# Attention pairs with pooled PSUM tiles, a reordered gate chain in the first expert layer, and one 512 column w2 operand in the second

## The chip, the cores and the metric

One core of a Trainium2 chip runs the whole program. The metric is the device time of one execution in microseconds (us), lower is better. Time before: 1605.31 us, the median of 3 runs (1603.46 to 1607.17).

## The reference

Three layers, all in float32. Attention over 4 batches of 2496 rows, with squared ReLU in place of softmax; then two mixture-of-experts layers over the 9984 rows that come out, each row going to the one expert of 8 with the largest logit.

```python
# attention: u, v (4, 2496, 256), z (4, 2496, 64)
attn = np.maximum(z @ z.transpose(0, 2, 1) / S, 0) ** 2
x = (u * (attn @ v)).reshape(B * S, D)
# layer 1: only rows with x @ w_skip > 0 are computed, the others pass through
e = argmax(xc @ w_gate);  g = softmax(xc @ w_gate)[e]
out = xc + g * (np.maximum(xc @ w1[e], 0) @ w2[e])       # w1 (8, 256, 1024), w2 (8, 1024, 256)
# layer 2: every row; logits get a bias by modality; no residual
out = g * (np.maximum(x @ w1[e], 0) @ w2[e])
```

## The kernel before, in words

To reach float32 accuracy on TensorE each operand is split into a high and a low part (`hh`, `hl`, `w2h`, `w2l`, `ah`, `al`, ...), and a product is three matmuls: high by high, high by low, low by high. ScalarE (ACT) makes the high part by a copy, VectorE (DVE) or GpSimd (POOL) subtracts it for the low part. The program orders the work of every engine by hand, and each engine runs its instructions in the order in which the code emits them.

**Attention.** A unit is two key tiles of 128 against a chunk of up to 512 queries; 4 batches of 5 chunks of 10 units make 200 units. In unit i TensorE does `scores` of unit i and `values` of unit i - 3 (`LAG`); ACT does ReLU (L285) and square (L297), DVE the cast (L298) and the low part (L299). `jobs` puts loads and splits of the next batch's z and v at written units. When a chunk's `values` are done, its `tail` generator runs one step a unit, emitted after the unit's own split and jobs: product with u, high and low part of the rows (`xh` L350, `xl` L351), four steps `rows(g)` that transpose the rows and multiply them by both gates on TensorE (L365) and copy the result out (L369, L373), then the argmax (`FirstMax`, `first_max_done`, L114 to L141), exp (L123), and the ranks: `row_index` has eight small matmuls (L153, L158, L163) that need the last sum of L141, and after DVE work the rows are scattered to lists in DRAM, one list per expert of either layer (L687). The small PSUM results live in `Banks`, one tile of two banks whose halves are handed out in turn.

**Expert layers.** `Moe1` takes 348 rows of one expert in a turn, `Moe2` 512. A turn (`turn`, `work`) is eight steps `hidden(f)` (six matmuls each, L767, then ReLU on ACT, L769, and the low part on DVE, L770) and eight steps `out_part(f)` (L868 in Moe1, L978 in Moe2). A plan, keyed ("h", f) or ("o", f), says what is emitted behind each step: "next" loads the next turn's rows and w1, "w1" b and "w2" b split a quarter of a weight (ACT, with DVE for w1 and POOL for w2, L672 and L673), "x" d transposes the next rows (L752), "after" runs one step of the generator that finishes the turn before. `Moe1.after` copies y out of PSUM (L878, L879), makes yl (L882), multiplies by the second gate (L886, L888), transposes y back and adds it to the rows (`x_out`, L895, L899), then does logits (L905), argmax, and ranks; `send` scatters `x_out` (three indirect DMAs on POOL, L687). POOL instructions `touch` (L709) take the waits for the DMAs; the one in `index` stands ahead of DVE's write of the row numbers `ix` (L713). `Moe2.out_part` has the 128 rows as the stationary operand and 256 columns of w2 as the moving one.

Of the kernel before, what the change touches and what calls it, by code (L numbers as in the profile page):

```python
# [183 lines left out]
class Attention:  # L184
# [51 lines left out]
    def z_split(self, b, i):  # L236
# [97 lines left out]
    def tail(self, b, c):  # L334
# [17 lines left out]
        yield  # L352

# [3 lines left out]
        def rows(g, lo=lo):  # L357

            ps = self.ps_m.both()
            q = slice(g * 128, g * 128 + 128)  # L360
            for d in range(2):
                cc = slice(64 * d, 64 * d + 98)
                for i, m in enumerate((xh, xl)):
                    for h, p in enumerate(HALVES):
                        nc.tensor.matmul(  # L365
                            ps[:, h, cc], m[p, d, q], self.wg[p, d, cc], start=(d == i == 0), stop=(d == i == 1),
                            skip_group_check=True,
                        )
# [45 lines left out]
    def run(self, first, inits, late):  # L414
# [32 lines left out]
        for b in range(nb):  # L447
# [4 lines left out]
            if b + 1 < nb:  # L452
                for i, (c, u) in enumerate(((1, 9), (2, 7), (2, 9), (3, 7), (3, 9))):
# [3 lines left out]
                for g, (c, u) in enumerate(((4, 5), (4, 7), (4, 9), (5, 4), (5, 6))):  # L457
# [155 lines left out]
class Banks:  # L613


    def __init__(self, pool):
        self.t, self.i = pool.tile([128, 2, 512], F32, name="m"), 0

    def both(self):
        return self.t  # L620

    def tile(self, shape, dtype, name):
        t = self.t[:shape[0], self.i]
        self.i = 1 - self.i
        if len(shape) == 2:
            return t[:, 0:shape[1]]
        return t[:, 0:shape[1] * shape[2]].rearrange("p (a b) -> p a b", a=shape[1])


class Shared:  # L630


    def __init__(self, ctx, tc, w):
# [9 lines left out]
        self.ps_m = Banks(pool("ps_m", 1, space=PSUM))  # L643
# [4 lines left out]
    def more(self, ctx):  # L648
# [3 lines left out]
        self.hi.append([p.tile([128, 2, 256], F32R, name=f"w2h{b}") for b in range(4)])  # L652
        self.lo.append([p.tile([128, 2, 256], F32R, name=f"w2l{b}") for b in range(4)])
# [70 lines left out]
class Moe:  # L724
# [68 lines left out]
    def turn(self, follow, after, hooks=None):  # L793
# [4 lines left out]
        def hook(what, *args):  # L798
# [10 lines left out]
            elif what == "x":  # L809
                nxt[0].x_transposed(args[0])  # L810
            elif what == "load w2":
# [12 lines left out]
class Moe1(Moe):  # L824
    PLAN = {
        "start": [("next",), ("after",)],
        ("h", 0): [("after",)],
        ("h", 1): [("after",)],
        ("h", 2): [("w2", 0)],
        ("h", 3): [("w2", 1)],  # L830
        ("h", 4): [("w2", 2), ("after",), ("after",)],
        ("h", 5): [("w2", 3), ("load w2",), ("after",)],
        ("h", 6): [("after",)],
        ("h", 7): [("after",)],
        ("o", 0): [("x", 0)],
        ("o", 1): [("w1", 0), ("after",)],
        ("o", 2): [("w1", 1)],
        ("o", 4): [("x", 1), ("w1", 2)],
        ("o", 5): [("w1", 3), ("after",)],
# [30 lines left out]
    def after(self, lim, current, ps=None):  # L870
# [17 lines left out]
        nc.scalar.copy(lt[:2 * E], lt_ps)  # L888
        yield
        x, xo = self.x_cur, self.x_out[:P]  # L890
        for g0 in range(0, G, 2):
# [10 lines left out]
            yield  # L902
        lg_ps = sh.ps_m.tile([128, G, 128], F32, name="m")[:P]
        for g in range(G):
            nc.tensor.transpose(lg_ps[:, g], lt[:, g * P:(g + 1) * P], k.ident)  # L905
        lo = s.tile([128, G, 2 * E], F32, name="mlo")[:P]
        nc.scalar.copy(lo, lg_ps[:, :, 0:2 * E])
        lg = s.tile([128, G, E], F32, name="mlg")[:P]
        nc.vector.tensor_tensor(lg, lo[:, :, 0:E], lo[:, :, E:], op=ALU.add)
        nc.vector.tensor_tensor(lg, lg, x[:, :, C_G1:C_G1 + 1].to_broadcast([P, G, E]), op=ALU.mult)  # L910
        nc.vector.tensor_tensor(lg, lg, x[:, :, C_B2:C_B2 + E], op=ALU.add)
        yield
        fm = FirstMax(nc, s, k, lg, P, G, "b")
        fm.exp()
        oh, sm = fm.hot, fm.total()
        nc.vector.tensor_copy(xo[:, :, C_TID], x[:, :, C_TID])
        nc.vector.reciprocal(xo[:, :, C_G2], sm)
        yield
        if current is not None:
            self.load_rows(current(), self.x_cur)  # L920
        nc.vector.tensor_copy(sh.lim, lim.rearrange("p t o -> p (t o)"))
        mk = self.counted(sh.lim)
        ohb, cum = first_max_done(nc, s, k, oh, mk, P, 1, G, "b")
        yield
        at, mk = row_index(nc, s, ps or sh.ps_m, k, ohb, cum, mk, self.carry, P, 1, G, "b")
        self.sc.index(at[:, 0], mk[:, 0])
# [11 lines left out]
class Moe2(Moe):  # L938
    PLAN = {
        "start": [("next",), ("after",)],  # L940
        ("h", 2): [("after",)],
# [20 lines left out]
    def take_y(self):  # L962
        self.y = [y[:, :D] for y in self.sh.y] + [self.sh.ps_m.tile([128, D], F32, name="m") for _ in range(2)]
# [238 lines left out]
```

## Time and profile before

| | |
|---|---|
| median of 3 runs | 1605.31 us |
| the profiled execution, its own time | 1608.57 us |
| its span from first to last instruction | 1606.8 us |
| busy: PE, weight loads, DVE, ACT, POOL | 1503.0, 1315.0, 1052.0, 940.8, 633.1 us |
| mean granted clock of TensorE | 0.982 |

PE is TensorE's matmuls, PEld its weight loads. Matmuls overlap, and their ends are modelled, so a busy PE can still have pauses of under 0.15 us. An arrow in a row names what ended a wait. SP is the queue that issues most loads.

### The profile page before, as it was taken

How to read it: one execution, taken by the hardware profiler on the slowest of the kernel's cores; microseconds unless marked ns; L12 is line 12 of the kernel's file. 1: busy time of each engine (PE TensorE's matmuls, PEld its weight loads, DVE VectorE, ACT ScalarE, POOL GpSimd, SP SyncE). 2: the span in 40 equal slices, each digit the busy share in tenths (PEclk: the TensorE clock that was granted, in tenths of full speed). 3: DMA queues.
4: the chain of work that ended last, by engine and by line, in shares of the span. 5: the costliest groups of instructions: out<-in, count | busy, mean ns of one | idle time of the engine just before them, and what ended most of it. 6: DMA issues, size and time to landing. Idle time of an engine off the chain costs nothing. (4 is left out here: it accounts for less than half of the span.)

```text
span 1606.8 us, 35550 instructions
## 1 busy us (share of the span) xinstructions
PE 1503.0 (94%) x11612; PEld 1315.0 (82%) x11612; DVE 1052.0 (65%) x2466; ACT 940.8 (59%) x1577; POOL 633.1 (39%) x740
## 2 busy tenths in 40 slices
PE   6999999999999999999779888889999999999996
PEld 4888887778888888888678887888989998998995
DVE  7688787878778787777656665656644454454442
ACT  7676777767677776665355444544454555455442
POOL 4222233333222222335444345553544544454453
PEclk9999999999999999999899999999999999999998
DMA  4611111112111110031355445553434433433430
GB/s 141 227 41 60 56 39 43 44 62 85 39 35 66 54 41 27 30 92 43 102 157 156 139 139 146 155 155 107 152 122 154 148 114 131 155 116 119 157 118 22
DMA packets 49694, 160.23 MB, mean 100 GB/s; under 512 B 13285, under 2 KB 15195, under 8 KB 40384
## 3 DMA queue, kind: packets, MB, share of 16 engines
q1 hardware_dynamic: 28432, 124.19, 24.6%
q0 software_dynamic: 20736, 34.71, 6.3%
q8 instruction: 61, 1.00, 0.3%
q14 instruction: 33, 0.27, 0.1%
q10 hardware_dynamic: 432, 0.07, 0.0%
HBM read 124.24 MB, written 46.55 MB: 106 GB/s over the span
## 5 line engine op out<-in xcount | busy, mean ns | idle before, releaser
L687 POOL DMA_INDIRECT rows<-r,ix x160 | 203.4, 1272 | 294.5 <-DVE ah L298 153.4
L328 PE MATMUL o<-ah,vh 64*128 64x512 f32 (+1 forms) x1560 | 312.7, 387 | 4.5 <-DVE xs L341 4.3
L770 DVE SCALAR_TENSOR_TENSOR hl<-ph,hh 128x512 fp32r<-128x512 f32 (+1 forms) x288 | 176.7, 615 | 213.9 <-ACT hh L769 212.9
L328 PE MATMUL o<-al,vh 64*128 64x512 f32 (+1 forms) x1560 | 305.5, 386 | 0.0
L328 PE MATMUL o<-ah,vl 64*128 64x512 f32 (+1 forms) x1560 | 304.1, 386 | 0.0
L285 ACT ACTIVATE t<-s 128x1024 f32<-128x1024 f32 (+2 forms) x201 | 200.7, 999 | 108.5 <-PE s L282 98.6
L769 ACT ACTIVATE hh<-ph 128x512 fp32r<-128x512 f32 (+1 forms) x288 | 155.1, 539 | 185.9 <-PE ph L767 172.2
L299 DVE TENSOR_TENSOR al<-t,ah 128x1024 fp32r<-128x1024 f32 (+2 forms) x201 | 244.6, 1217 | 18.3 <-PE m L365 0.5
L673 POOL TENSOR_TENSOR w2l<-w2raw,w2h 128x512 fp32r<-128x512 f32 x144 | 183.4, 1288 | 169.5 <-issue 132.2
L767 PE MATMUL ph<-mxh,zA 128*128 128x512 f32 (+1 forms) x576 | 217.4, 377 | 10.0 <-PEq L1198 5.6
L298 DVE CAST ah<-t 128x1024 fp32r<-128x1024 f32 (+2 forms) x201 | 140.2, 697 | 113.3 <-ACT t L297 111.0
L767 PE MATMUL ph<-mxh,zB 128*128 128x512 f32 (+1 forms) x576 | 212.0, 368 | 0.0
L767 PE MATMUL ph<-mxl,zA 128*128 128x512 f32 (+1 forms) x576 | 211.9, 368 | 0.0
L297 ACT ACTIVATE t<-t 128x1024 f32<-128x1024 f32 (+2 forms) x201 | 208.0, 1035 | 5.7
L328 PEld LDWEIGHTS o<-ah,vh 64*128 64x128 f32 x1560 | 152.1, 187 | 37.7 <-DVE xs L341 8.7
L328 PEld LDWEIGHTS o<-al,vh 64*128 64x128 f32 x1560 | 151.9, 186 | 27.7
L328 PEld LDWEIGHTS o<-ah,vl 64*128 64x128 f32 x1560 | 148.3, 186 | 28.5
L767 PEld LDWEIGHTS ph<-mxh,zA 128*128 128x128 f32 x576 | 110.7, 192 | 25.4 <-issue 8.2
L282 PE MATMUL s<-zA,zB 64*128 64x512 f32 (+1 forms) x400 | 124.7, 390 | 0.0
L282 PE MATMUL s<-zB,zA 64*128 64x512 f32 (+1 forms) x400 | 122.9, 390 | 0.0
L767 PEld LDWEIGHTS ph<-mxh,zB 128*128 128x128 f32 x576 | 110.3, 192 | 14.8
L767 PEld LDWEIGHTS ph<-mxl,zA 128*128 128x128 f32 x576 | 110.6, 192 | 13.9
(235 smaller groups left out, 3274.1 us busy)
## 6 DMA issues: line engine op xcount, KB each, us to landing
w1raw<-in_w SPq DMA_DIRECT2D x36, 1024.0 KB, 7.6
w2raw<-in_w SPq DMA_DIRECT2D x36, 1024.0 KB, 9.5
x_in<-rows SPq DMA_DIRECT2D x20, 520.0 KB
vraw<-in_v SPq DMA_DIRECT2D x20, 512.0 KB, 4.0
ut<-in_uT SPq DMA_DIRECT2D x20, 512.0 KB, 4.8
x_in<-rows SPq DMA_DIRECT2D x16, 364.3 KB
x_cur<-rows SPq DMA_DIRECT2D x16, 364.3 KB
rows<-x_in POOLq DMA_DIRECT2D x8, 536.0 KB, 8.2
```

What stands on the lines that cost most here:

```text
L282: nc.tensor.matmul(s[:, i, :n], w[p, k], x[p, q], start=(j == 0), stop=(j == 2))
L285: nc.scalar.activation(t[:, i, :n], s[:, i, :n], AF.Relu, scale=SCALE)
L297: nc.scalar.activation(t[:, i, :n], t[:, i, :n], AF.Square)
L298: nc.vector.tensor_copy(h[:, i, :n], t[:, i, :n])
L299: nc.vector.tensor_tensor(l[:, i, :n], t[:, i, :n], h[:, i, :n].bitcast(F32), op=ALU.subtract)
L328: nc.tensor.matmul(o[half][d][:, :n], w[p, d * 128:d * 128 + 128], x[p, :n], start=(u == 0 and j == at[0]), stop=(u == 9 and j == at[-1]),)
L673: lo_engine.tensor_tensor(l, src, h.bitcast(F32), op=ALU.subtract)
L687: i = tc.nc.gpsimd.indirect_dma_start(out=out, out_offset=bass.IndirectOffsetOnAxis(ap=ix, axis=0), in_=rows, in_offset=None, bounds_check ...
L767: nc.tensor.matmul(ps, w, x, start=(i == 0), stop=(i == len(mms) - 1))
L769: nc.scalar.activation(h, ps, AF.Relu)
L770: nc.vector.scalar_tensor_tensor(l, ps, 0.0, h.bitcast(F32), op0=ALU.max, op1=ALU.subtract)
```

## The change

- Attention: the copy of the last 64 columns of z goes from ACT to DVE. The tail gets an empty step ahead of `rows`, so all that follows comes a unit later; exp, ranks and the index now stand in one step, with the sums, reciprocals and scatters in the next. `Banks` is gone: `ps_m` is a pool of two one-bank tiles, and each `rows(g)` is copied out by four ACT copies in place of two. Four of five splits of z and three of v move to an earlier unit, one of v to a later one.
- Moe1: `after` has the gate chain (lt, logits, argmax, exp, ranks, index) first, then the transposes of y and the rows. y stays in PSUM longer: yl is computed from it, and the copies to `yS` follow the lt matmuls. `send` leaves the start of the turn for ("h", 3) of the next one; w2 quarters 0 and 1 are split at ("o", 6) and ("o", 7) of the turn before, 2 and 3 at ("h", 1) and ("h", 2), and the load of the next w2 follows there.
- Moe2: w2's high and low part lie side by side, so one matmul of 512 columns takes both for `hh`, and a second of 256 columns adds `hl` by the high part to the upper half. `after` then adds the two halves with four more DVE instructions.

```diff
-                nc.scalar.copy(t[:, S:S + 64], t[:, S - 64:S].bitcast(F32))
+                nc.vector.tensor_copy(t[:, S:S + 64], t[:, S - 64:S].bitcast(F32))
...
         yield
+        yield
...
-            ps = self.ps_m.both()
+            ps = [self.ps_m.tile([128, 196], F32, name="m") for _ in HALVES]
...
-            nc.scalar.copy(
-                r[:, g, 0:D].rearrange("p (d h c) -> p h d c", d=2, h=2),
-                ps[:, :, 0:196].rearrange("p h (d c) -> p h d c", d=2)[:, :, :, 0:64],
-            )
-            nc.scalar.copy(lo[:, :, g], ps[:, :, 64:98])
+            to = r[:, g, 0:D].rearrange("p (d h c) -> p d h c", d=2, h=2)
+            for h, t in enumerate(ps):
+                nc.scalar.copy(to[:, :, h], t.rearrange("p (d c) -> p d c", d=2)[:, :, 0:64])
+                nc.scalar.copy(lo[:, h, g], t[:, 64:98])
...
         fm.exp()
-        yield
-        sm = fm.total()
         at, mk = row_index(nc, self.p_s, self.ps_m, k, ohb, cum, mk, self.carry, 128, 2, 4, "a")
...
+        yield
+        sm = fm.total()
...
-                for i, (c, u) in enumerate(((1, 9), (2, 7), (2, 9), (3, 7), (3, 9))):
+                for i, (c, u) in enumerate(((1, 8), (2, 5), (2, 8), (3, 5), (3, 8))):
...
-                for g, (c, u) in enumerate(((4, 5), (4, 7), (4, 9), (5, 4), (5, 6))):
+                for g, (c, u) in enumerate(((4, 5), (4, 6), (4, 8), (5, 5), (5, 7))):
...
 class Moe1(Moe):
     PLAN = {
         "start": [("next",), ("after",)],
         ("h", 0): [("after",)],
-        ("h", 1): [("after",)],
-        ("h", 2): [("w2", 0)],
-        ("h", 3): [("w2", 1)],
-        ("h", 4): [("w2", 2), ("after",), ("after",)],
-        ("h", 5): [("w2", 3), ("load w2",), ("after",)],
+        ("h", 1): [("after",), ("w2", 2)],
+        ("h", 2): [("w2", 3), ("load w2",)],
+        ("h", 3): [("send",), ("after",)],
+        ("h", 5): [("after",)],
         ("h", 6): [("after",)],
         ("h", 7): [("after",)],
-        ("o", 0): [("x", 0)],
-        ("o", 1): [("w1", 0), ("after",)],
-        ("o", 2): [("w1", 1)],
-        ("o", 4): [("x", 1), ("w1", 2)],
-        ("o", 5): [("w1", 3), ("after",)],
+        ("o", 0): [("x", 0), ("after",)],
+        ("o", 1): [("w1", 0)],
+        ("o", 2): [("after",), ("w1", 1)],
+        ("o", 3): [("after",)],
+        ("o", 4): [("after",), ("x", 1), ("w1", 2)],
+        ("o", 5): [("w1", 3)],
+        ("o", 6): [("w2", 0)],
+        ("o", 7): [("w2", 1)],
     }
...
         for d in range(2):
-            nc.scalar.copy(y[:, d], self.y[d])
             nc.scalar.copy(yh[:, d], self.y[d])
         for d in range(2):
             yield
-            nc.vector.tensor_tensor(yl[:, d], y[:, d], yh[:, d].bitcast(F32), op=ALU.subtract)
+            nc.vector.tensor_tensor(yl[:, d], self.y[d], yh[:, d].bitcast(F32), op=ALU.subtract)
...
         nc.scalar.copy(lt[:2 * E], lt_ps)
+        for d in range(2):
+            nc.scalar.copy(y[:, d], self.y[d])
         yield
...
     with tc.For_i(0, n, 1, iteration_sync=mode) as j:
-        m1.send()
         m1.turn(lambda: m1.next(j), m1.finish(j))
...
 class Moe2(Moe):
...
-            for i, (h, w) in enumerate(((self.hh, wh), (self.hl, wh), (self.hh, wl))):
-                nc.tensor.matmul(
-                    self.y[g][:P], h[f][:, gg], w, start=(f == 0 and i == 0), stop=(f == 7 and i == 2)
-                )
+            nc.tensor.matmul(
+                self.y[g][:P], self.hh[f][:, gg], w.rearrange("p t d -> p (t d)"), start=(f == 0), stop=False
+            )
+            nc.tensor.matmul(self.y[g][:P, D:], self.hl[f][:, gg], w[:, 0], start=False, stop=(f == 7))
...
+        for g in range(G):
+            if g % 2 == 0:
+                yield
+            nc.vector.scalar_tensor_tensor(
+                self.o[:P, g], self.y[g][:P, D:], old[:P, g, 0:1], self.o[:P, g], op0=ALU.mult, op1=ALU.add
+            )
```

The plans of the turns that are not in a loop follow the same order.

## Rows read from the trace of the kernel before

**Rows 1.** Busy time by stage: start:end us, length, engines, granted clock, DMA share, GB/s

```profile
0.00:752.60 752.60, 719.29 (x6646) 595.35 (x6646) 592.46 (x1223) 533.23 (x732) 232.72 (x211) 0.99 0.19 64
...
812.70:1093.70 281.00, 242.14 (x1535) 229.36 (x1535) 175.15 (x585) 139.79 (x326) 131.50 (x169) 0.98 0.50 147
1093.70:1141.90 48.20, 44.80 (x289) 40.06 (x290) 33.82 (x112) 23.41 (x50) 23.64 (x33) 1.00 0.39 134
1141.90:1554.00 412.10, 412.10 (x2635) 373.22 (x2635) 199.18 (x393) 207.59 (x388) 194.97 (x259) 1.00 0.41 134
```

**Rows 2.** Waits of PE, whole span: us in total, times, longest us

```profile
PE m L895 <- DVE x_out L899: 26.2, 14, 3.6
PE s L282 <- ACT t L285: 15.6, 7, 3.8
PE m L895 <- ACT mlt L888: 14.0, 16, 1.0
PE m L365 <- DVE xl L351: 7.6, 25, 0.7
...
PE m L153 <- DVE mxl L757: 6.5, 3, 5.5
```

**Rows 3.** Waits of all engines, the two behind those of PE

```profile
DVE x_out L899 <- DMA rows<-x_out,ix_scatter: 28.8, 13, 4.6
...
ACT zA L248 <- DVE zA L244: 14.0, 4, 3.6
```

**Rows 4.** Stretches before and in a drop of the granted clock, columns as in rows 1

```profile
161.00:163.00 2.00, 0.04 (x5) 0.00 (x0) 0.58 (x1) 1.36 (x5) 0.00 (x0) 1.00 0.00 0
163.00:166.50 3.50, 3.49 (x18) 2.90 (x20) 2.35 (x6) 2.81 (x3) 0.00 (x0) 0.51 0.00 0
...
907.10:910.60 3.50, 2.88 (x12) 2.81 (x13) 1.47 (x4) 0.37 (x1) 1.21 (x2) 0.51 0.40 87
```

**Rows 5.** Timeline of one tail's ranks, DVE and PE: start, duration, instruction

```profile
229.34 0.21 DVE L114 TENSOR_REDUCE mxa<-lg 128x8 f32<-128x64 f32 x1
...
231.18 0.77 DVE L141 TENSOR_TENSOR cuma<-cuma,ohba 128x16 bf16<-128x16 bf16 x4
231.20 0.39 PE L282 MATMUL s<-zA 64*128 64x512 f32 x1
...
234.60 0.20 PE L153 MATMUL m<-ohba,tri 64*128 64x64 bf16 x2
```

**Rows 6.** Groups by line, ACT copies of rows: count, busy us, mean ns, idle before

```profile
L369 ACT COPY r<-m 128x256 f32<-128x256 f32 x80 | 29.8, 372 | 46.5 <-PE m L365 45.5 <-issue 0.4
L373 ACT COPY lo<-m 128x68 f32<-128x68 f32 x80 | 17.8, 223 | 0.0
```

**Rows 7.** Timeline of one loop turn of Moe1, begun at 833.69, all engines

```profile
839.22 1.27 POOL L687 DMA_INDIRECT rows<-x_out,ix_scatter  x1 [0.18 <-PE m L886]
...
840.51 4.98 POOL L673 TENSOR_TENSOR w2l<-w2raw,w2h 128x512 fp32r<-128x512 f32 x4
...
842.10 0.48 DVE L899 SCALAR_TENSOR_TENSOR x_out<-m,x_cur 116x256 f32<-116x256 f32 x1 [2.27 <-DMA rows<-x_out,ix_scatter]
...
843.77 0.43 PE L895 MATMUL m<-ident,yS 128*116 128x128 f32 x2 [1.99 <-DVE x_out L899]
```

**Rows 8.** The tile x_out: its scatters, from issue to landing

```profile
DMA to landing us min/median/max: 4.0/4.4/5.0
```

**Rows 9.** The line of the splits, DVE: ns min/median/max, first and last start

```profile
L673 DVE TENSOR_TENSOR zB<-w1raw,zA x140: 678/685/1434, 772.2 to 1563.6; 128x512 fp32r<-128x512 f32 x140
```

**Rows 10.** DMA issues of the page: KB each, median us to landing

```profile
w2raw<-in_w SPq DMA_DIRECT2D x36, 1024.0 KB, 9.5
```

**Rows 11.** Timeline of PE in Moe2: neighbours of 256 columns, then of 512

```profile
1306.09 0.28 PE L978 MATMUL m<-w2h,hh 128*128 128x256 f32 x1
1306.21 0.28 PE L978 MATMUL m<-w2h,hl 128*128 128x256 f32 x1
...
1309.26 0.39 PE L767 MATMUL ph<-mxh,zA 128*128 128x512 f32 x1
1309.49 0.40 PE L767 MATMUL ph<-mxl,zA 128*128 128x512 f32 x1
```

More of the change, by code (lines that the diff above doesn't have):

```diff
@@ L651, in more @@
         p = self.p = pool("moe", 1)
-        self.hi.append([p.tile([128, 2, 256], F32R, name=f"w2h{b}") for b in range(4)])
-        self.lo.append([p.tile([128, 2, 256], F32R, name=f"w2l{b}") for b in range(4)])
+        self.w2hl = [p.tile([128, 2, 2, D], F32R, name=f"w2{b}") for b in range(4)]
+        self.hi.append([t[:, :, 0] for t in self.w2hl])
+        self.lo.append([t[:, :, 1] for t in self.w2hl])
         self.hh = [p.tile([128, 512], F32R, name=f"hh{f}") for f in range(8)]
@@ L810, in hook @@
                 nxt[0].x_transposed(args[0])
+            elif what == "send":
+                self.send()
             elif what == "load w2":
@@ L888, in after @@
         nc.scalar.copy(lt[:2 * E], lt_ps)
+        for d in range(2):
+            nc.scalar.copy(y[:, d], self.y[d])
         yield
         x, xo = self.x_cur, self.x_out[:P]
+        lg_ps = sh.ps_m.tile([128, G, 128], F32, name="m")[:P]
+        for g in range(G):
+            nc.tensor.transpose(lg_ps[:, g], lt[:, g * P:(g + 1) * P], k.ident)
+        lo = s.tile([128, G, 2 * E], F32, name="mlo")[:P]
+        nc.scalar.copy(lo, lg_ps[:, :, 0:2 * E])
+        lg = s.tile([128, G, E], F32, name="mlg")[:P]
+        nc.vector.tensor_tensor(lg, lo[:, :, 0:E], lo[:, :, E:], op=ALU.add)
+        nc.vector.tensor_tensor(lg, lg, x[:, :, C_G1:C_G1 + 1].to_broadcast([P, G, E]), op=ALU.mult)
+        nc.vector.tensor_tensor(lg, lg, x[:, :, C_B2:C_B2 + E], op=ALU.add)
+        yield
+        fm = FirstMax(nc, s, k, lg, P, G, "b")
+        yield
+        nc.vector.tensor_copy(sh.lim, lim.rearrange("p t o -> p (t o)"))
+        mk = self.counted(sh.lim)
+        ohb, cum = first_max_done(nc, s, k, fm.hot, mk, P, 1, G, "b")
+        yield
+        fm.exp()
+        yield
+        at, mk = row_index(nc, s, sh.ps_m, k, ohb, cum, mk, self.carry, P, 1, G, "b")
+        self.sc.index(at[:, 0], mk[:, 0])
+        yield
         for g0 in range(0, G, 2):
@@ L901, in after @@
                 )
[L902 to L915, printed above, removed]
+            if g0 == 0:
+                yield
         nc.vector.tensor_copy(xo[:, :, C_TID], x[:, :, C_TID])
-        nc.vector.reciprocal(xo[:, :, C_G2], sm)
-        yield
+        nc.vector.reciprocal(xo[:, :, C_G2], fm.total())
         if current is not None:
             self.load_rows(current(), self.x_cur)
[L921 to L926, printed above, removed]
     def send(self):
@@ L940 @@
         "start": [("next",), ("after",)],
+        ("h", 0): [("after",)],
+        ("h", 1): [("after",)],
         ("h", 2): [("after",)],
@@ L962, in take_y @@
     def take_y(self):
-        self.y = [y[:, :D] for y in self.sh.y] + [self.sh.ps_m.tile([128, D], F32, name="m") for _ in range(2)]
+        self.y = self.sh.y + [self.sh.ps_m.tile([128, 2 * D], F32, name="m") for _ in range(2)]
     def x_transposed(self, d):
@@ L992, in after @@
         for g in range(G):
-            nc.scalar.activation(self.o[:P, g], self.y[g][:P], AF.Copy, scale=old[:P, g, 0:1])
+            nc.scalar.activation(self.o[:P, g], self.y[g][:P, :D], AF.Copy, scale=old[:P, g, 0:1])
+        for g in range(G):
+            if g % 2 == 0:
+                yield
+            nc.vector.scalar_tensor_tensor(
+                self.o[:P, g], self.y[g][:P, D:], old[:P, g, 0:1], self.o[:P, g], op0=ALU.mult, op1=ALU.add
+            )
         yield
@@ L1080, in forward_kernel @@
         "start": [("next",), ("after",)],
+        ("h", 0): [("after",)],
         ("h", 2): [("after",)],
@@ L1136, in forward_kernel @@
         "start": [("after",)],
-        ("h", 0): [(lambda: m2.table.spread(nc, sh.ps_x, k),), ("next",)],
+        ("h", 0): [("after",), (lambda: m2.table.spread(nc, sh.ps_x, k),), ("next",)],
     })
```

54 lines of the change are left out of this document (22 added, 32 removed).

## The prediction

> **What bounds the kernel now.** I read the busy time by stage first [rows 1]. PE is busy 719 of 753 us in attention, 412 of 412 in Moe2's stage, but only 242 of 281 in the 13 loop turns of Moe1; DVE, the next engine, has 592, 199 and 175. So PE sets the time everywhere, and an edit is worth what it takes from PE's own work or from PE's waits. The list of PE's waits [rows 2] says where the waits are: those on `x_out` and `mlt` are Moe1's (40 us together), those on `t` and `xl` attention's (23 us). Behind them [rows 3] stand the scatter that must have read `x_out` before it is written again, and ACT's wait of about 3.5 us for DVE in each of the four z splits. Last I looked at the granted clock [rows 4]: after 2 us without a matmul at 161 it is 0.51, the level of 1.2 GHz, for 3.4 us, which costs 1.7 us. I count such stretches: four in attention (37, 163, 347, 532), each behind a wait of PE of 2 to 4 us, and four in Moe1's loop (907, 931, 996, 1081).
>
> **Attention, what goes.** The copy of z's last columns on DVE: ACT no longer stands 3.5 us in its queue ahead of the next ReLU, for which PE waits [rows 2, 3]. At the three changes of batch that is 2.0 us of wait and 1.7 us of slow clock each, 11 us; in batch 0 the wait is the longest row, 3.8, of which I take 3.3 (another split stays in ACT's queue there) and 1.7, so 5 us. DVE's two copies of 64 columns are small beside its 1.2 us subtractions. The empty step gives `xl` a whole unit more: all 25 waits of L365 go, 7.6 us by the row, 8 as ends are modelled. Sum -24. The four ACT copies for two: by the two rows [rows 6] a copy is about 0.17 us plus 0.8 ns a column, so 0.93 us for 0.60 a step, 80 steps, 27 us of ACT. ACT is at 533 of 753, and the copies fall into the 1.1 us in which it waits for the next scores: nothing. If that cover went, it would be up to 0.3 us a step, 27 us.
>
> **Attention, what comes.** Between the argmax and the rank matmuls the old tail has two units of PE work, the new one has one. In the tail of [rows 5] the argmax starts at 229.34, which is ReLU, square, cast and subtraction behind the unit's start, and its last sum ends at 231.95; PE is at the place of the rank matmuls, one unit earlier than today's 234.60, at 231.20. So PE, in order, stands 0.75 us, and 0.06 for the release. I took the same difference at 18 tails: 0.72 to 1.22 us, more where a split of z or v falls just ahead, as it now does in four of five chunks. Mean 1.0, 19 tails, +19 us. Queued behind are the next unit's scores, and ACT, DVE behind these. The bounds: 0, if DVE ran the argmax earlier than I think, and 2.7 us a tail if each stall brought the slow clock. Waits of PE for `xs` of up to 0.85 us brought none, so I take the stall alone. Attention: -5.
>
> **Between attention and the experts** the two early transposes of Moe1's rows now take a small PSUM tile between two `rows` steps, and the next of these waits for DVE's `mxl`: some 2.2 us, perhaps with a slow stretch; the wait of L153 for `mxl` [rows 2] stays in part. +4 (0 to 8).
>
> **Moe1's loop.** 281.0 us by 13 turns is 21.6 [rows 1]. PE's own work is 242.1 / 13 = 18.6, and 18.1 without the four slow stretches (6.8 us). The wait of 1.9 us a turn is that for `x_out` [rows 2, 7]: the rows are sent at the turn's start, the third scatter goes out at 839.22, 5.5 us into the turn, and `x_out` is written again from 842.10, so DVE waits, and PE's second pair of transposes with it. The other, 0.9, is the transposes behind `mlt`. In the new order the rows are written behind ("o", 3), some 9 us after the send, and the transposes of `lt` come two steps after its matmuls: both waits go. What is late next is the send itself. POOL must first do w2 quarters 2 and 3, 1.25 us each [rows 7], behind ACT's copies for ("h", 1) and ("h", 2): low parts done at 4.4 and 5.6 us into the turn, touches 1.1, scatters at 6.7, 8.6 and 10.3, and the last lands 4.4 to 5.0 us later [rows 8], at 14.7 to 15.3. The index step, behind ("o", 2) at 12.5, has a POOL touch that waits for it, and DVE waits for the touch. DVE's queue behind: w1 quarter 1 (0.69), three `x_out` (0.48), the sums and small copies (0.7), `mxl` (0.52): done at 18.4, when the next turn needs it at 18.1 + 0.6. So it just fits; two w1 quarters are still to do, and these meet w2 quarters 0 and 1 on POOL. The DVE split takes 685 ns, but up to 1434 [rows 9], and 18 of 140 take twice the time, those beside POOL's subtraction of w2. That is up to 1.5 us more in DVE's queue, of which the low parts of the next turn's hidden steps can pass on part to PE through three PSUM tiles. I take 18.5 us a turn, from 18.1 (nothing passed on) to 20.
>
> SBUF — State Buffer, section Who interferes with whom, in the Trainium skill, says that a DVE instruction with two SBUF inputs contends with a GpSimd instruction that reads SBUF; the doubled split times agree. It speaks against the new place of quarters 0 and 1: by it both splits would be doubled in each turn, and if all of that reached PE it would be 13 x 1.5 = 20 us, about the first rival's time.
>
> The load of w2 goes out at 5.6 and takes 9.5 [rows 10]: 15.1, and it is needed at 16.7. Loop: 13 x 18.5 and 1.9 for leaving it, 242.4, so -38.6. The two turns behind the loop have 48.2 - 44.8 = 3.4 us of idle PE [rows 1]: -3.4.
>
> **Moe2.** Each pair of a row group and a quarter step is now 512 + 256 columns for 3 x 256. Neighbours stand 0.12 us apart at 256 columns and 0.23 at 512 [rows 11]: 0.35 for 0.36. 32 pairs in 20 turns, 640 in all, by some 8 ns: -5 us. The bounds: 512 columns at twice 0.12 give 0; at 2.4 GHz without any extra they take 0.213, -17 us. The saved weight loads are hidden behind matmuls today. The four DVE additions (about 0.48 each as for `x_out` [rows 7], 1.9 a turn) go to DVE at 199 of 412: nothing, but +0.5 in the last turn, where nothing follows.
>
> TensorE: Matmul & The Clock Gate, section Back-to-back issue gap, in the Trainium skill, gives N / 2.4 + 2.5 ns from one matmul to the next. That is 109 and 216 ns where the trace has 120 and 230; by it the pair would save 2.5 ns, 1.6 us in all.
>
> **The sum.** -5 + 4 - 38.6 - 3.4 - 5 + 0.5 = -47.5. The profiled execution took 1608.6, so 1561; it was 3.3 above the median, so against 1605.3 I say **1558 us**.
>
> **Rivals.**
> - *The send is the new bound of Moe1.* Landing and the doubled splits make a turn 20.3. For it: the margin I find is a few tenths. Against: 4.4 us is a narrow row. 13 x 1.8 more: 1581. Chance 0.13.
> - *The rank stalls pull the clock down.* 19 x 1.7 = 32 more: 1590. For: PE stands once a chunk. Against: nothing of 0.85 us did it. 0.06.
> - *No rank stall*, as DVE is early: 19 less, 1539. For: DVE has one step less to do in a unit. Against: [rows 5]. 0.10.
> - *Slower than before.* The one way that I see: the scatters land behind the w2 load, which now runs beside them, and the touch holds DVE until a turn is over 22.2 us, that is a landing 3.7 us later than 15. Each us costs 13, and from there the loop gives back all; at 22.5 it is 1610. Against: today's w1 load runs beside the scatters too, and they land in 5.0 at most. 0.06.
> - *The wide operand gives nothing*: 512 columns cost twice 256. 1563, inside my forecast's own range, 1545 to 1572, which has 0.62.
> - No change at all, several things cancelling: 0.03.
>
> The range reaches to the first rival and nearly to the third: 1536 to 1586. A measurement of this kernel tells about 0.2% from no change. Faster 0.90, same 0.03, slower 0.07.
>
> **What would show it.** The waits of L365 for `xl` and of L248 gone, and the clock full at the batch changes; a new wait of PE at L153 of about 1 us, 19 times. Loop turns of 18 to 19 us without waits at L895; a wait of DVE at L713 or of POOL's touch for the scatter near 13 to 15 us into the turn. L978 at 0.23 and 0.12. Wrong I am if DVE's queue in Moe1 passes its lateness on to L767, or if the slow clock follows the new stalls.

## The result: slower by 1%, and the profile after

| | before | after |
|---|---|---|
| median | 1609.1 us (8 runs, 1603.5 to 1616.6) | 1623.4 us (8 runs, 1620.9 to 1626.5) |
| ratio | | 1.0101, 95% interval 1.0081 to 1.0121 |
| span of the profiled execution | 1606.8 us | 1619.1 us |
| mean granted clock of TensorE | 0.982 | 0.975 |

I had forecast 1558 us, 1536 to 1586. The time lies outside the range, and on the other side of no change.

The stages of the changed kernel, by windows cut at the same places of the program as in [rows 1] (columns as there):

```profile
0.00:748.50 748.50, 720.01 (x6646) 606.97 (x6646) 602.70 (x1231) 541.34 (x876) 231.10 (x211) 1.00 0.20 64
748.50:811.90 63.40, 45.28 (x262) 41.27 (x262) 38.47 (x124) 23.77 (x64) 29.97 (x33) 0.84 0.35 101
811.90:1100.90 289.00, 246.01 (x1534) 235.03 (x1535) 191.60 (x585) 140.83 (x326) 130.85 (x169) 0.95 0.51 144
1100.90:1153.30 52.40, 47.77 (x256) 42.21 (x257) 36.03 (x113) 22.07 (x48) 23.43 (x33) 0.92 0.38 127
1153.30:1565.40 412.10, 409.40 (x2092) 345.34 (x2091) 224.47 (x464) 206.30 (x388) 192.89 (x257) 1.00 0.40 134
```

Against [rows 1], attention is 4.1 us shorter and Moe1's loop 8.0 us longer, where I had 38.6 shorter. The two turns ahead of the loop take 63.4 for 60.1 us, the two behind it 52.4 for 48.2, Moe2's stage the same 412.1. With 0.9 us more at the end, that is the 12.3 us between the spans. So the bulk of the miss is Moe1's loop: 289.0 us for the 242.4 of the prediction, 46.6 us too long. All that lies outside the loop comes out 13.2 us above its forecasts.

PE's waits over the whole span of the changed kernel, beside [rows 2]:

```profile
PE m L737 <- DMA x_in<-rows: 29.8, 13, 4.7
PE ph L752 <- DVE mxl L742: 13.1, 7, 2.0
PE ph L752 <- PEq L1202: 12.2, 2, 7.6
PE m L158 <- DVE cuma L141: 8.1, 20, 0.4
PE s L282 <- ACT t L285: 7.8, 7, 2.6
PE m L153 <- DVE cuma L139: 6.7, 8, 4.0
...
PE m L153 <- DVE cumb L139: 3.3, 1, 3.3
PE m L366 <- DVE mxl L742: 3.3, 1, 3.3
...
PE m L366 <- DVE xl L351: 0.2, 1, 0.2
```

Moe1's two old waits (`x_out` 26.2, `mlt` 14.0) are gone, as forecast. In their place PE waits for the next rows: 29.8 us for the load of `x_in` and 13.1 for the low part of such rows. In the loop alone (813 to 1101) the list is this, 43.1 us in all:

```profile
PE m L737 <- DMA x_in<-rows: 20.9, 11, 2.5
PE ph L752 <- DVE mxl L742: 13.1, 7, 2.0
PE ph L752 <- PEq L1202: 7.6, 1, 7.6
PE ph L752 <- DVE hl L755: 1.5, 3, 0.5
```

The clock adds to it. In the loop TensorE stands at the lower of its two levels, 1.2 GHz, for 29.1 us in eight stretches (from 812, 846, 891, 935, 966, 1021, 1065 and 1096), each of them in or behind one wait of PE of 2.0 to 7.6 us; in the kernel before it is 13.7 us in four. This is the stretch at 891, behind a wait of 2.5 us:

```profile
890.90:894.30 3.40, 3.40 (x16) 3.33 (x15) 1.21 (x2) 1.71 (x4) 0.00 (x0) 0.50 0.41 146
```

By the price of [rows 4], 1.7 us for 3.4, that is an estimate of 14.5 us, for 6.8 before.

Who is behind the waits stands in the list of all engines' waits (L694 is the POOL touch, L698 DVE's write of the index):

```profile
POOL ix_scatter L694 <- DMA rows<-x_out,ix_scatter: 80.8, 15, 7.0
...
ACT zA L657 <- DMA w1raw<-in_w: 25.0, 15, 8.9
DVE ix_scatter L698 <- POOL ix_scatter L694: 24.9, 14, 2.4
```

The touch waits for the scatters' landing, and DVE waits for the touch, 1.8 us a turn. The turns of the loop alternate: six take 19.2 to 21 us and seven 21.7 to 26.7, the last of which leaves the loop. One of the shorter, begun at 855.39, and the start of the next (begun at 875.93), from the timeline:

```profile
858.67 2.54 POOL L658 TENSOR_TENSOR w<-w2raw,w 128x512 fp32r<-128x512 f32 x2 [0.78 <-issue]
...
861.44 0.34 SPq L649 DMA_DIRECT2D w2raw<-in_w  x1
...
865.79 1.27 POOL L672 DMA_INDIRECT rows<-x_out,ix_scatter  x1 [0.19 <-issue]
...
874.09 0.18 POOL L694 TENSOR_TENSOR ix_scatter<-ix_zero_scatter 1x3 int32<-1x3 int32 x1 [7.03 <-DMA rows<-x_out,ix_scatter]
874.31 0.16 DVE L698 TENSOR_TENSOR ix_scatter<-atb,mk 116x3 int32<-116x3 f32 x1 [2.20 <-POOL ix_scatter L694]
875.02 1.26 DVE L912 SCALAR_TENSOR_TENSOR x_out<-m,x_cur 116x256 f32<-116x256 f32 x3
876.89 0.31 SPq L730 DMA_DIRECT2D x_cur<-rows  x1
879.53 0.30 SPq L730 DMA_DIRECT2D x_in<-rows  x1
...
890.41 0.49 PE L737 MATMUL m<-ident,x_in 116*128 116x116 f32 x3 [2.46 <-DMA x_in<-rows]
```

The third scatter goes out at 10.4 us into the turn (I had 10.3) and lands 8.1 us later, at 18.5 (I had 14.7 to 15.3); the touch that waits for it starts at 18.7. In the other turns the third scatter goes out at 10.4 to 13.9 us, later in most of the longer ones, whose first steps wait for the low part of their rows, and the touch starts at 17.1 to 20.9. DVE writes the index 2.2 us late, so the sums of `x_out` come late, so `x_cur`, which they read, is loaded late. On SP `x_in` stands behind `x_cur`: it goes out 3.6 us into the next turn, where PE wants it at its first output step and stands 2.5 us. The scatters of `x_out` from issue to landing, beside [rows 8]:

```profile
DMA to landing us min/median/max: 4.1/7.5/9.5
```

The busy share of the 16 transfer engines in tenths, in 40 slices over the 24 us from the start of a turn (the turn and the start of the next), first in the kernel before (942.5 on), then in the changed one (855.4 on):

```profile
DMA  2969999966746321000009589983122222259899
```

```profile
DMA  1022222999999999999887532222200000000311
```

The share over the loop is the same (0.50 and 0.51), but before it came in bursts apart: w1 and the scatters first, w2 in the middle, the rows' loads at the end. Now `x_in`, w1, w2 and the scatters share one burst of some 9 us, and then the engines are idle for 5.

### The profile page after: what moved, and what is told of

Its sections match the earlier page's. It is cut to its first block, busy times and chain, and to the rows that moved or that the text cites. A ratio compares the mean times of both kernels' runs of the same rounds, so it can differ in the third digit from the quotient of the medians.

```text
span 1619.1 us, 34652 instructions
## 1 busy us (share of the span) xinstructions
PE 1505.8 (93%) x10972; PEld 1301.7 (80%) x10972; DVE 1111.8 (69%) x2554; ACT 949.0 (59%) x1729; POOL 632.3 (39%) x740
## 5 line engine op out<-in xcount | busy, mean ns | idle before, releaser
L672 POOL DMA_INDIRECT rows<-r,ix x160 | 202.6, 1266 | 269.1 <-DVE xs L341 205.9
L658 POOL TENSOR_TENSOR w<-w2raw,w 128x512 fp32r<-128x512 f32 x144 | 187.3, 1311 | 249.5 <-issue 153.8
L752 PE MATMUL ph<-mxh,zA 128*128 128x512 f32 (+1 forms) x576 | 216.3, 375 | 21.2 <-PEq L1202 12.2
L752 PE MATMUL ph<-mxl,zA 128*128 128x512 f32 (+1 forms) x576 | 213.9, 371 | 13.1 <-DVE mxl L742 13.1
L298 DVE CAST ah<-t 128x1024 fp32r<-128x1024 f32 (+2 forms) x201 | 146.5, 729 | 97.9 <-ACT t L297 94.7
L328 PEld LDWEIGHTS o<-ah,vl 64*128 64x128 f32 x1560 | 151.9, 185 | 24.7
L741 ACT CAST mxh<-m 128x512 fp32r<-128x512 f32 (+1 forms) x72 | 37.8, 525 | 176.0 <-PE m L737 170.4
L858 PE MATMUL o<-hh,w 128*128 128x348 f32 x512 | 137.1, 352 | 0.5 <-POOL w L658 0.5
L658 DVE TENSOR_TENSOR zB<-w1raw,zA 128x512 fp32r<-128x512 f32 x140 | 114.8, 840 | 28.7 <-ACT zA L657 23.1
```

Source lines behind the costliest of these rows:

```text
L298: nc.vector.tensor_copy(h[:, i, :n], t[:, i, :n])
L328: nc.tensor.matmul(o[half][d][:, :n], w[p, d * 128:d * 128 + 128], x[p, :n], start=(u == 0 and j == at[0]), stop=(u == 9 and j == at[-1]),)
L658: lo_engine.tensor_tensor(l, src, h.bitcast(F32), op=ALU.subtract)
L672: i = tc.nc.gpsimd.indirect_dma_start(out=out, out_offset=bass.IndirectOffsetOnAxis(ap=ix, axis=0), in_=rows, in_offset=None, bounds_check ...
L741: nc.scalar.copy(self.xh[:, d], ps)
L752: nc.tensor.matmul(ps, w, x, start=(i == 0), stop=(i == len(mms) - 1))
```

## The experiments

"Loop" is the time from the first hidden matmul of Moe1's loop to the first one behind it, in each run's profile: 280.9 in the kernel before, 289.0 in the changed one.

| run | loop, us | total, us | ratio to before, 95% interval |
|---|---|---|---|
| e1_send_start | 277.5 | 1616.6 (one run; before 1604.8) | |
| e2_xcur_late | 317.9 | 1670.9 (one run) | |
| e3_ix_copy | 269.4 | 1597.2 (one run) | |
| e4_rank_later | 289.2 | 1621.5 (one run) | |
| e5_x_in_first | 269.1 | 1618.9 | 1.0092 (1.0064 to 1.0119) |
| e6_no_moe1 | 273.9 | 1597.9 | 0.9951 (0.9930 to 0.9973) |
| e7_w2_quarter | 259.4 | 1588.4 (one run; before 1606.5) | |
| e8_rows_first | 266.5 | 1595.4 | 0.9937 (0.9916 to 0.9959) |
| e9_rows_first_ix | 266.9 | 1590.4 | 0.9897 (0.9871 to 0.9922) |
| e10_w2_tail_dve | 241.3 | 1569.4 | 0.9773 (0.9730 to 0.9816) |
| e11_w2_all_dve | 244.0 | 1567.9 | 0.9759 (0.9718 to 0.9800) |
| e12_w2_tail_only | 262.7 | 1594.1 | 0.9955 (0.9926 to 0.9985) |

**The send back at the turn's start.**

```diff
-        "start": [("next",), ("after",)],
+        "start": [("send",), ("next",), ("after",)],
-        ("h", 3): [("send",), ("after",)],
+        ("h", 3): [("after",)],
```

> The changed kernel with one edit: Moe1's send stands at the start of the turn again, ahead of w2 quarters 2 and 3 on POOL; all else stays. Theory A (the late send is the cause: its scatters land 18 us into the turn, hold POOL's touch and DVE behind it, and DVE then holds the loads of x_cur and x_in on SP): the scatters land by 11 us, DVE's wait for the touch goes, x_in's load goes out some 4 us earlier, and a loop turn takes 18.2 to 19 us in place of 22.2; the whole about 45 us less than the changed kernel, 1575 to 1585. Theory B (the order of loads on SP is the cause: x_in's load stands behind x_cur's and shares the queues with w1 and w2): PE still waits for x_in at L737, at least 1.5 us a turn, and a turn takes 20 to 21 us, 1595 to 1605.

The loop fell by 11.5 us. The waits for `x_in` fell to 12.2 us (3.5 of them in the loop), but PE now waited 22.9 us at the ranks (L153) for DVE's `cumb`, 13 times. So the lateness of the send is part of the loss, not all of it, and neither forecast was met: something else made DVE late. What, showed only later (below).

**The load of x_cur behind the next x_in and w1.** In the plan ("cur" loads `x_cur`, which the end of `after` no longer does):

```diff
-        "start": [("next",), ("after",)],
+        "start": [("next",), ("cur",), ("after",)],
```

> The changed kernel with one edit: the load of x_cur stands behind the next turn's loads of x_in and w1 on SP, at the start of the turn after, in place of ahead of them. Theory A: the waits of L737 for x_in (29.8 us) go, but DVE is still held by the touch until 18 us into the turn, so the waits of L752 for mxl (13 us) stay or grow: a loop turn of 20 to 21 us, 1600 to 1610 in all. Theory B: nothing else holds the loop, a turn takes 18.2 to 19 us, 1575 to 1585.

The waits for `x_in` went (9.2 us are left), and the loop grew to 317.9. The waits of DVE from 853 to 1040, and of PE:

```profile
DVE mlg L891 <- DMA x_cur<-rows: 35.7, 7, 5.4
```

```profile
PE m L153 <- DVE cumb L139: 71.5, 14, 18.4
PE m L737 <- DMA x_in<-rows: 9.2, 2, 4.7
```

The change puts the logits, which read `x_cur`, at ("h", 5), ahead of the rows. So `x_cur` is needed early in a turn while its one buffer comes free at the end of the turn before. Each order of the two loads makes one of them late; that is a wait that the new gate chain itself brings, and the prediction did not have it.

**The index in a tile of its own, no touch.** DVE writes a second tile (in `index`), and POOL copies it at the send (in `send`).

```diff
-        self.touch(self.ix, self.zero, self.zero)
-        self.nc.vector.tensor_tensor(self.ix[:self.P], a, b, op=ALU.add)
+        self.nc.vector.tensor_tensor(self.new[:self.P], a, b, op=ALU.add)
...
-        self.touch(self.ix, self.ix, self.zero)
+        self.nc.gpsimd.tensor_copy(self.ix, self.new)
```

> The changed kernel with one edit: in Moe1 the index step writes a second tile, with no touch ahead of it, and the send copies it to the tile that the scatters read. DVE no longer waits for the scatters at the index. Theory A: DVE then waits for the same landing one step later, at the first write of x_out (L912), so the loop turn stays within 0.7 us of 22.2 and the whole within 10 us of the changed kernel. The touch alone as the cause: a turn of 19 to 20 us, 30 to 40 us less.

19.6 us off the loop, between the two forecasts. DVE's wait did not move to `x_out` (1.2 us in all): by then the scatters had landed. `x_in` still cost PE 30.7 us (21.0 in the loop).

**Exp and ranks in separate steps again** (attention).

```diff
         fm.exp()
+        yield
         at, mk = row_index(nc, self.p_s, self.ps_m, k, ohb, cum, mk, self.carry, 128, 2, 4, "a")
         ix = self.p_s.tile([128, 2, 4], I32, name="ix")
         nc.vector.tensor_tensor(ix, at, mk, op=ALU.add)
-        yield
         sm = fm.total()
```

> The changed kernel with one edit, in attention's tail: exp in a step of its own again, ranks, sums and scatters together in the step after, so two units of PE work lie between the argmax and the rank matmuls as in the kernel before, and the empty step stays. If PE's new stall at the ranks costs what its rows say (8.1 + 6.7 us of waits at L158 and L153, about 1 us a tail from one matmul's start to the next), attention ends 16 to 19 us earlier and the whole takes 1604 to 1608. If the stall only stands in for waits that come anyway, the gain is under 5 us.

Attention ended at 746.4 for 748.5, 2.1 us earlier, so the stall mostly stands in for a wait that comes anyway. The waits at the ranks were gone, but a wait that the changed kernel has once stood in their place:

```profile
PE o L328 <- DVE xs L341: 18.7, 18, 1.8
```

I read it as DVE being late in these units as a whole, with the rank stall as the place where it shows; no run tests that.

**x_in first, then x_cur, then w1** (with the index copy).

```diff
-        "start": [("next",), ("after",)],
+        "start": [("next", 0), ("cur",), ("load w1",), ("after",)],
```

> The changed kernel with the index written to a tile of its own (as in the run with the index copy), and the order of the loads on SP turned: the next rows x_in first, then x_cur, then w1. Theory C (after the touch, what is left is that x_in stands behind x_cur on SP, and x_cur behind the last sums of x_out): x_in is issued some 2.5 us before the turn ends, as in the kernel before, PE's 31 us of waits for x_in in the run with the index copy are gone, x_cur lands some 5 us into the turn, before the logits need it at about 8, and a loop turn is 18.5 to 19.2 us: loop 242 to 252, total 1570 to 1580. Theory D (it is the bulk of bytes: x_in, x_cur, w1, w2 and the scatters now all fall into the same half of a turn, and whichever comes last holds someone): the wait moves to x_cur's landing (the logits on DVE, then the ranks on PE) or to w1's, and the loop stays at 262 to 270, total 1590 to 1598.

The loop stayed at 269.1, as theory D has it: no waits for `x_in`, but 27.3 us of DVE's logits for `x_cur` and 15.7 us of PE at the ranks (805 to 1060). The total was worse since the two turns behind the loop took 75.3 us; that comes after the loop, and I did not follow it up.

**All but Moe1's new order.** The kernel before with attention's part, the `ps_m` pool, the w2 tile and `Moe2` of the changed one; `Moe1.PLAN`, `Moe1.after` and the places of `send` as before.

> The kernel before with all of the change but Moe1's new order: attention's part, the small PSUM tiles and the w2 operand of 512 columns in Moe2. If the stages are independent: attention ends 4 us earlier (748.5), Moe1's loop stays at 281 with turns of 20.4 to 24, Moe2's turn goes from 23.57 to 23.30 (-5.4 over 20), so 1596 to 1599 beside 1605 to 1609: both of these parts together are worth some -9 us, and Moe1's part alone made the changed kernel slower. Rival: the shared pieces (two small PSUM tiles for one double one, w2's high and low parts side by side) are themselves what slows Moe1: then its loop is over 285 here too, with longer splits of w2 on ACT or POOL or waits for the m tiles, and the total is 1605 or more.

1597.9, faster by 0.5%, so Moe1's new order alone turns a gain into a loss of 1%. The first hidden matmul comes at 749.8 and Moe2's turn takes 23.3. The loop, 273.9, is shorter by 7 than before, in the old order. PE's waits in it, but for those at its start and its exit, are down to one row:

```profile
PE m L890 <- DVE x_out L884: 28.8, 13, 4.0
```

So the waits on `mlt`, 11.7 us in this loop before, are gone without the new order. The one edit of this run that bears on them is the pool: the transposes of y no longer share a PSUM tile with the result that ACT copies to `mlt`. That is argued from the list, as no run changes the pool alone. The clock takes some of it back, with 23.9 us at the lower level for 13.7.

**A quarter of w2.** Only the first quarter of w2's columns is loaded.

```diff
-        self.nc.sync.dma_start(self.raw[i], w.rearrange("o p w -> p (o w)")[:, i * 2048:(i + 1) * 2048])
+        m = 512 if i and not isinstance(e, int) else 2048
+        self.nc.sync.dma_start(self.raw[i][:, :m], w.rearrange("o p w -> p (o w)")[:, i * 2048:i * 2048 + m])
```

> The changed kernel with only a quarter of w2 loaded for every expert but the first (512 of 2048 columns; the rest of the raw tile keeps old values), all instructions else the same. If the scatters land late because w2's load runs beside them: the last of them lands 4.4 to 5.5 us after its issue, not 8, the POOL touch is done before DVE comes to it, DVE's waits at the index (25 us in the loop) are under 5, x_cur and x_in go out 2 us earlier, and the loop is 252 to 265. If the landing hangs on w1, x_in or on the number of scatters' own packets, it stays at 7 to 8 us and the loop at 283 to 289.

Met: loop 259.4, 29.6 us less, with every instruction in its place. The scatters' landing:

```profile
DMA to landing us min/median/max: 4.2/4.7/5.7
```

So in the changed kernel the late landing comes from w2's load beside the scatters. It is not w2 alone that can do it: in the run with the early send w2's load goes out some 4 us behind the third scatter, with `x_in` and w1 some 6 us ahead of it, and the median landing is 7.3 us. Turns of 19.0 to 20.3 us, and 24.6 for the one that leaves the loop, were left, with 13.0 us of waits for `x_in` in all (805 to 1060): without the late landing my 18.5 would still have been some 1 us short.

**The rows ahead of the ranks** (with the early send).

```diff
         fm.exp()
         yield
-        at, mk = row_index(nc, s, sh.ps_m, k, ohb, cum, mk, self.carry, P, 1, G, "b")
-        self.sc.index(at[:, 0], mk[:, 0])
-
-        yield
         for g0 in range(0, G, 2):
...
             self.load_rows(current(), self.x_cur)
+        yield
+        at, mk = row_index(nc, s, sh.ps_m, k, ohb, cum, mk, self.carry, P, 1, G, "b")
+        self.sc.index(at[:, 0], mk[:, 0])
```

> The changed kernel with the send at the turn's start and, in the turn, the rows x_out written ahead of the rank matmuls and the index (they change places; x_cur's load goes out with the rows). Theory E (in the run with the early send the loads were spread again, and what was left was PE's 1.8 us a turn for the ranks, because DVE's small operations of the logits stood while POOL subtracted w2's quarters): with the ranks two steps later these waits of PE go, x_cur and x_in go out 1 to 1.5 us earlier, the touch does not wait since the scatters land by 14 us: a loop turn is 18.6 to 19.4, the loop 243 to 255, total 1580 to 1592. Rival F: x_out is now written at about 14.5 us into the turn, when the last scatter has just landed (13 to 14): DVE waits for it or the sums are late, PE waits at the row transposes or at the ranks in the end, and the loop stays at 268 to 278.

Between the two: loop 266.5. The waits for `x_in` went (0.4 us from 805 to 1060), as E has it; but PE still stood 19.4 us at the ranks, now behind DVE's sums. E was right on the loads and wrong on the ranks.

**The same with the index copy, and the first early transpose a unit later.** The edits are those of the index copy and, in the list of late jobs:

```diff
-            (8, lambda: m1.x_transposed(0, spare())),
+            (9, lambda: m1.x_transposed(0, spare())),
```

> The same as the run with the rows first, with the index in a tile of its own that POOL copies at the send (no touch in the index step), and the two early transposes of Moe1's first rows each one unit apart from before (unit 9 for the first). Theory E: the touch does not wait any more, so the index copy gives nothing beyond 3 us in the loop; the stall of 3.3 us near 734 and its slow clock go or shrink if it came from the small PSUM tile between two row steps: -2 to -4 in attention; total 1577 to 1592, 0 to 7 less than with the rows first alone. Rival F: if the touch is what waits at the end of the turn, the copy takes 1 us a turn, 13 us, off.

The copy gave the loop nothing (266.9). Attention ended 2.6 us earlier than in the changed kernel, 745.9. And its timeline shows what makes DVE late (POOL and DVE in one turn):

```profile
914.65 1.27 POOL L672 DMA_INDIRECT rows<-x_out,ix_scatter  x1 [0.18 <-issue]
914.74 0.17 DVE L897 TENSOR_TENSOR mlg<-mlo 116x24 f32<-116x24 f32 x1
915.01 3.52 DVE L898 TENSOR_TENSOR mlg<-mlg,x_cur 116x24 f32<-116x24 f32 x1
915.94 2.54 POOL L658 TENSOR_TENSOR w<-w2raw,w 128x512 fp32r<-128x512 f32 x2
918.56 0.18 DVE L899 TENSOR_TENSOR mlg<-mlg,x_cur 116x24 f32<-116x24 f32 x1
```

An operation on 24 columns, 0.18 us elsewhere, takes 3.52 and ends 0.05 us behind POOL's second subtraction of w2. Eleven of the 13 loop turns have such a row, of 2.2 to 3.5 us, on this line or the one above it, each ending 0.05 us behind POOL's pair. With the early send alone it is 12. Eight of the eleven had begun 0.7 to 0.9 us ahead of the pair, as the one above; why they had not ended by then no run shows.

**w2's quarters 2 and 3 on DVE, later in the turn.** On top of the run before; "w2v" is the split "w2" with DVE in place of POOL.

```diff
-        ("h", 1): [("after",), ("w2", 2)],
-        ("h", 2): [("w2", 3), ("load w2",)],
+        ("h", 1): [("after",)],
         ("h", 3): [("after",)],
-        ("h", 5): [("after",)],
+        ("h", 4): [("w2v", 2)],
+        ("h", 5): [("after",), ("w2v", 3), ("load w2",)],
```

> The run with the rows first and the index copy, with w2's quarters 2 and 3 subtracted by DVE behind ("h", 4) and ("h", 5) in place of POOL behind the scatters. Theory G (what is left there, 1.7 us a turn of PE's wait at the ranks, comes from DVE's small operations of two SBUF inputs in the logits, which take 3.3 us in place of 0.18 when POOL's two subtractions run, until these end): no such operation over 1 us in the loop, the wait at the ranks under 0.5 us a turn, a turn of 18.6 to 19.2 us, loop 244 to 254, total 1567 to 1578. Theory H (DVE's queue as a whole is the bound, and it gets 1.4 us more a turn): the ranks wait 1 us or more all the same, or PE waits for hl, and the loop stays at 260 to 269, total 1583 to 1592.

Loop 241.3, 3 us better than theory G had it. The last turn, the one that leaves the loop, takes 23.3, and the others from the second on 17.9 to 18.6. The same line of the logits over the whole run has no long one any more (its ns are minimum, median, maximum):

```profile
L900 DVE TENSOR_TENSOR mlg<-mlg,x_cur x16: 184/184/203, 792.0 to 1084.4; 116x24 f32<-116x24 f32 x16
```

The busy share of the transfer engines, as above, from the start of a turn (883.9 on), shows the loads apart again, `x_in` and w1 with the scatters first and w2 behind them:

```profile
DMA  2222287899998563598999963000122222228989
```

The waits of PE are down to those at the loop's start (L1125) and exit (L1212) and 1.5 us at the ranks (805 to 1060):

```profile
PE ph L761 <- PEq L1212: 4.6, 1, 4.6
PE ph L761 <- DVEq L1125: 3.5, 1, 3.5
PE m L153 <- DVE x_out L919: 1.5, 3, 0.5
```

Two things changed at once here, the engine and, through the later splits, the time of w2's load; the timeline above says that the first freed DVE, and the next run but one bears on the second.

**All four quarters on DVE.** The plan has "w2v" 0 to 3 behind ("h", 1), ("h", 2), ("h", 4) and ("h", 5).

> The same with all four quarters of w2 on DVE, behind ("h", 1), ("h", 2), ("h", 4) and ("h", 5), so that POOL subtracts nothing in the loop. Theory G: the doubled times of w1's splits (1.1 us a turn) go as well, and DVE has 1.4 us more in the hidden steps, where it waits 2.7 us a turn for ACT: a turn of 18.3 to 19 us, loop 240 to 252, total 1565 to 1577. Theory H: hl or the logits come late by 1 to 2 us a turn, PE waits for hl (L761 of the run with the rows first and the index copy) or at the ranks, and the loop is 258 to 272.

1567.9, the fastest, 2.4% under the kernel before; from the run before it by less than these runs tell. The doubled w1 splits are gone, but the loop is 244.0 for 241.3, so that gained nothing there. The scatters land later (median 9.3 us for 6.5) and PE waits 4.1 us for `x_in`, so other losses may hide what the splits cost; no run separates them.

**Only w2's quarters moved** in the changed kernel, the send left at ("h", 3), with the touch.

```diff
-        ("h", 1): [("after",), ("w2", 2)],
-        ("h", 2): [("w2", 3), ("load w2",)],
+        ("h", 1): [("after",)],
         ("h", 3): [("send",), ("after",)],
-        ("h", 5): [("after",)],
+        ("h", 4): [("w2v", 2)],
+        ("h", 5): [("after",), ("w2v", 3), ("load w2",)],
```

> The changed kernel with one thing moved: w2's quarters 2 and 3 are subtracted by DVE behind ("h", 4) and ("h", 5), in place of POOL behind ("h", 1) and ("h", 2), and w2's load follows there. The send stays at ("h", 3), the touch in the index step, x_cur ahead of x_in. Theory J (the place of these two quarters and of the load behind them is what cost the changed kernel its gain: POOL gets to the send some 2.5 us sooner, and the scatters no longer share the transfer engines with w2's load): the scatters go out at some 4.5 to 8 us and land by 14, the touch waits under 1 us for DVE, x_in is in before PE wants it or at most 1 us late, a turn is 18.2 to 19.6 us, loop 242 to 256, total 1572 to 1586. Rival K (the touch and the order of x_cur, x_in and w1 cost as much by themselves): the touch or x_in still hold a turn at 20 to 21 us, loop 262 to 275, total 1592 to 1605.

26.3 us off the loop, and the changed kernel becomes faster than the one before, by 0.5%. By the loop it is K's 262 to 275, by the waits J's: the touch holds DVE 5.7 us in all, `x_in` PE 6.0 and its low part PE 6.1 (805 to 1060). J's mechanism was half wrong: the scatters still take 8.2 us to land (median), as w1 and `x_in`, and w2 from some 9.5 us on, run beside them, but they go out some 3 us sooner, at about 3.8, 5.5 and 7.7 us into the turn.

## Why the prediction was wrong

**The step that failed** is the one that begins "What is late next is the send itself" and ends "So it just fits". Its times up to the third scatter hold in the turn shown (10.4 for 10.3); the mean of the 13 turns is 11.8. The landing was mis-sized: 4.4 to 5.0 us from [rows 8], 7.5 by the trace after, so the touch starts at 17.1 to 20.9 us where I had 15. The rows that I used were taken beside a w1 load that had gone out 6 us ahead of the third scatter. The change puts `x_in`, w1 and w2 beside the scatters, and I used w2's load only for when w2 itself arrives. The quarter of w2 shows it: 4.7 us, and 29.6 us off the loop.

The rival that I called the one way to be slower has this mechanism: the scatters land behind w2's load, and the touch holds DVE. I gave it 0.06, on the argument that a load runs beside the scatters today too. Its price came out by luck. It has a turn of 22.2 us as the one from which the loop gives back all, and 289.0 / 13 is 22.2; by my own sum that is no change, 1605 us. The kernel is slower because what lies outside the loop adds 13.2 us to its forecasts.

**What the step left out.** First, `x_cur` and `x_in` are one chain on SP: a late sum of `x_out` is a late `x_in` (20.9 us of PE's waits in the loop, and I looked for a wait at L713 or the touch alone). Second, the logits at ("h", 5) need `x_cur` early; the two runs that turned the loads round show that it can't go behind. Third, where the send is early, POOL's subtractions of w2 stop DVE's small operations. I weighed POOL's w2 against DVE's splits, at up to 1.5 us a turn. The rule that I quoted from the Trainium skill, SBUF — State Buffer, section Who interferes with whom, covers this case too, and the trace agrees that the two contend; here the price was 3.3 us for an operation of 0.18, as it ended only behind the second of two subtractions in a row, and it lay on the gate chain. The changed kernel itself has no such row, so this is no part of its 46.6 us. Fourth, the sum has PE's work without slow stretches of the clock; the new waits brought eight, some 14.5 us by the price of [rows 4]. Leaving the loop cost PE 7.6 us, where the sum has 1.9.

**What held in Moe1.** PE's own work, 18.1 to 18.5 us a turn, was the right floor. The loop of the run with w2's quarters on DVE takes 241.3 us, where I had 242.4 for the changed kernel. The waits on `mlt` went as forecast, but by the run without Moe1's new order the pool does that, and not the order as I had it. No single cause owns the 46.6 us: less w2 gives 29.6, w2's quarters elsewhere 26.3, no touch 19.6, an early send 11.5. They overlap; the send, the rows, the touch and two quarters changed together give 47.7, and not every smaller set was run.

**Attention**, with what lies between it and the loop, was forecast -5 and +4 and measured -4.1 and +3.3. The sum is right, its terms are not. The waits of ACT's `t` fell from 15.6 to 7.8 us and those for `xl` from 7.6 to 0.2, and the four slow stretches of the clock in attention are gone, as forecast (one new one is below). PE waits 14.8 us at the ranks (8.1 and 6.7), 10.4 of it in attention, for my 19, without a slow clock, so the rival without rank stalls falls. But as a cost my 19 was far too much, since attention ends only 2.1 us earlier without these waits; that the sum still came out is luck. The early transposes did what I feared, once:

```profile
733.31 0.51 DVE L742 TENSOR_TENSOR mxl<-m,mxh 128x348 fp32r<-128x348 f32 x1
733.88 0.28 PEld L366 LDWEIGHTS m<-wg_split,xh 64*128 64x128 f32 x1 [3.38 <-DVE mxl L742]
```

```profile
730.50:733.80 3.30, 0.13 (x1) 0.00 (x0) 3.20 (x7) 1.12 (x2) 0.00 (x0) 1.00 0.00 0
733.80:737.30 3.50, 3.42 (x21) 3.42 (x23) 0.85 (x6) 1.63 (x6) 0.21 (x1) 0.51 0.02 5
```

That is 3.3 us of wait and 3.5 us at the clock's lower level, 5 us for my 4. The 3.3 us more between attention and the loop are in the main the first rows (waits for `x_in` of 9.0 us for 6.6) and 3.4 us more at the lower level.

**Behind the loop** I had -3.4; it was +4.2. PE stands 3.3 us at the ranks (L153 for `cumb`) in the second of these turns. The clock is at its lower level for 3.4 us behind that wait and for 5.0 us behind the loop's exit (0.92 in that window for 1.00).

**Moe2**: forecast -5; a turn fell from 23.57 to 23.30, 0.27 by 20 turns is -5.4. The pair as I had it, 0.23 and 0.12:

```profile
1309.16 0.40 PE L974 MATMUL o<-w,hh 128*128 128x512 f32 x1
1309.39 0.28 PE L977 MATMUL o<-w,hl 128*128 128x256 f32 x1
1309.51 0.39 PE L974 MATMUL o<-w,hh 128*128 128x512 f32 x1
```

One early turn took 27.8 us, since PE waited 2.7 us for `hl` and ran at the clock's lower level for 3.4 us behind it, and that gave the stage's gain back.

## What to carry to other kernels

A step moved earlier or later takes its transfers along: lay the turn's loads and stores on one time line before using a landing time from the old order, since a landing time measured beside one load is no price beside three. When a store's landing gates an index, a buffer and then the next load on the same queue, a few us become a loop in which every second turn is late. And keep a long POOL subtraction away from the short DVE operations, with two inputs in SBUF, of a chain that PE waits for, even if neither engine is busy on the mean. Last, count the clock: the new waits brought eight stretches at its lower level, some 14.5 us of the loop's 289.0.

## What the runs showed of the hardware that was not expected

- A DVE `tensor_tensor` on 116 x 24 elements with both inputs in SBUF took 2.2 to 3.6 us in place of 0.18 in 11 or 12 of the 13 loop turns of three runs, where POOL's pair of 128 x 512 subtractions began up to 1.0 us behind its start or up to 0.4 us ahead of it; it always ended about 0.05 us behind the pair.
- The same indirect scatter lands after 4.4 us (median) beside one load, 7.5 beside three, 4.7 when one of the three is cut to a quarter, and 7.3 where the third load follows 4 us behind the scatters.
- SP issues `x_in` 2.64 us behind `x_cur` (876.89 and 879.53), and 2.6 to 2.7 us in the changed kernel's loop from its second turn on, with no other load between them; why is open.
- Leaving the loop cost PE one wait of 7.6 us on its own queue (L1202) in the changed kernel, 4.6 and 4.2 in the two fastest ones, 1.1 in the kernel before.
